# ELU sums, low halves and every second gated product moved off VectorE, and a list scheduler with longer waits, in a top-k attention and two-MLP kernel

## The chip, the cores and the metric

The kernel runs on one core of a Trainium2 chip. The metric is the device time of one execution in microseconds (us). The program has five instruction streams that run side by side and meet only through semaphores: TensorE (PE in the profile; its weight loads are shown apart as PEld), VectorE (DVE), ScalarE (ACT), GpSimd (POOL) and SyncE (SP), which here only issues DMA transfers.

## The reference

Attention that keeps the 32 largest scores of each row, over 4 batches, 8 heads, 576 tokens and a head size of 64, then two MLPs on the 2304 tokens:

```python
scores = scale * q @ k.T
kth = np.partition(scores, -32, axis=-1)[..., -32:-31]
scores = np.where(scores >= kth, scores, -1e9)
attn = softmax(scores)                 # with 1e-9 added to the sum
x = (attn @ v) -> (2304, 512)
h = x @ w_in                           # 512 -> 2048
g = np.where(h > 0, h, np.exp(np.minimum(h, 0)) - 1)     # ELU
x = g @ w_out                          # 2048 -> 512
a, b = x @ w1, x @ w2                  # 512 -> 1024, twice
out = ((a * b) @ w3) @ w_out2          # 1024 -> 1024 -> 512
```

All values are float32.

## The kernel before

**Tiling.** The tokens go in 18 tiles of 128 rows, two tiles to a chunk, so nine chunks (`CHUNKS`). For each chunk there is an attention part and an MLP part; the MLP part of chunk c runs beside the attention part of chunk c+1. After the last attention only the rest of the MLP work is left. Matrix products are made from 16-bit halves: a value is stored as a high half and a low half, and each product takes three matmuls (high by high, high by low, low by high).

**Attention.** For each pair of heads and each tile (72 times) there are: the scores on TensorE (L376, four matmuls for a head, into one PSUM tile `psS`), their copy by ScalarE (L382), the search for the 32nd largest on VectorE (for each head four MAX8, L389, and three MATCH_REPLACE, L392), the masked exponential on ScalarE (L409, L411), the probabilities split into halves by ScalarE (L426) and GpSimd (L427), a transposing DMA (`pt<-pi`), the product with V on TensorE (L442, 28 matmuls), its scaling on VectorE (L447, `xf`, 8 for a chunk), a split by ScalarE (L449) and GpSimd (L450), and a transposing DMA into `x`, the chunk's input to the MLP.

**MLP.** On TensorE a chunk has eight A units (L674 to L676, 24 matmuls of 256 columns each), eight O units (L711 to L713, 24 each), a Y step (the result of O leaves PSUM in halves, L723 and L724, and small matmuls L731 and L736 find its scale), eight B units (L753 to L755, 24 each) and two D units (L788 to L790, 24 matmuls of 512 columns each, the output rows). Between A and O stands the ELU: ScalarE makes Relu(-h) and its exponential (L686, L687), GpSimd subtracts one and scales (L689), and then one of two ways joins the positive branch: VectorE takes the maximum with the PSUM tile (L691), or ScalarE makes a second Relu from PSUM (L695) and GpSimd adds it (L696). ScalarE and GpSimd split the result (L697, L698). In a B unit the two products a and b lie in one PSUM bank; ScalarE copies a (L772) and VectorE multiplies it by b from PSUM (L773), and after every second unit ScalarE and GpSimd split the pair (L778, L779). A second way through the B unit is in the code but not used: ScalarE copies both a and b (L763) and GpSimd multiplies them (L770).

**Weights.** All weights are loaded and unpacked at the start (L474 to L481), and w3 is multiplied by w_out2 on TensorE (L614, 64 matmuls), which gives `w34`. Each of the 56 weight tiles is then converted to a high half by ScalarE (L503) and a low half in one of three ways (`convert`): VectorE alone (mode D, L506), ScalarE scaling in place and GpSimd subtracting (mode G, L509 and L510), or two matmul steps on TensorE (L515 and L516) and a copy by ScalarE (mode P, L518). `conv_modes` takes from `PAR['cd']` how many tiles of a weight go by D and by G; the rest go by P.

**Order.** The order of the instructions on each engine is made when the program is built. Every operation is put in a list (`Program.op`) with an engine, a cost in ns and a priority. `emit` plays the list through: on each engine it takes the ready operation with the lowest rank, where the rank is the priority less `cpw` times the longest path of costs and waits behind the operation:

```python
rank = [o[4] - PAR["cpw"] * cp[i] for i, o in enumerate(self.ops)]
...
rt[s] = max(rt[s], end + (0.0 if e == "SP" else LAT.get((eng, self.ops[s][0]), 130.0)))
```

`LAT` is the wait in ns from the end of an operation on one engine to the start of one on another. On the chip each engine runs its own queue in this order and waits for what its next instruction needs, even when a later one is ready.

Of the kernel before, what the change touches and what calls it, by code (L numbers as in the profile page):

```python
# [36 lines left out]

# [112 lines left out]
def kernel(ctx: ExitStack, tc: tile.TileContext, qd, kd, vd, vn, w_in, w_out, w1, w2, w3t, w4, out,  # L150
# [5 lines left out]
    op = P.op  # L156
# [118 lines left out]
    def norm(pieces, dst, key, pr, kind="rot"):  # L275
# [65 lines left out]
    def attention(c, t0, n):  # L341
# [4 lines left out]
        for pair in range(4):  # L346
            for t in range(n):
# [14 lines left out]
                for hh in range(2):  # L362
# [4 lines left out]
                    for bi, b in enumerate(bs):  # L367
# [51 lines left out]
                for hh in range(2):  # L419
# [81 lines left out]
    def convert(W, nm, i, st, skeys, s, sk, pr, sid, kind="y"):  # L501
# [15 lines left out]
        op("PE", 1080, rest, [*skeys, (nm, i), ("si", sid), "ident"], [pk], pr)  # L517
        op("ACT", 480, lambda: A.activation(lo(W[i]), ps, AF.Copy), [pk], [(nm, i, "l")], pr)  # L518
# [76 lines left out]
    def prep_34(pr):  # L595
# [6 lines left out]
        def part(m):  # L602
# [53 lines left out]
    def mlp(c, t0, n, dprev, pr0, span, hooks=None):  # L656
        xs, vb = c % NXS, batch(t0 + n)
        X = XS[xs]
        N = n * 128
        nm = N / 2.4 + 3.0  # L660
        pr_of = lambda u: pr0 + u * span / 28.0
# [120 lines left out]
        def unitD(t, pr):  # L782
            rs = nxt("rot", 3)
            for q in range(4):
# [128 lines left out]
```

## Time and profile before

| | |
|---|---|
| device time, 3 runs | median 1086.86 us (1085.69 to 1093.07) |
| the profiled execution | 1089.24 us, its span 1087.5 us |
| busy in the span | PE 984.1 us, DVE 921.6, ACT 834.9, POOL 661.2 |
| mean granted TensorE clock | 0.968 of full speed |

The profile is of one execution. The span runs from the first to the last instruction of the program; the device time of the same execution is 1.74 us longer. A matmul's own time in the trace (0.27 us for 256 columns) overlaps with the next ones, since the array works as a pipeline, so TensorE's work is read from the step from one start to the next, not from the durations.

### The profile page before, as it was taken

The numbers are of one execution on the slowest core, as the hardware profiler recorded it, in microseconds if no ns is written. First come the engines' busy times: TensorE is split into PE (matmuls) and PEld (weight loads), VectorE is DVE, ScalarE is ACT, GpSimd is POOL, SyncE is SP. The second block draws the span as 40 slices with busy tenths as digits, with TensorE's granted clock in tenths as the row PEclk, the third lists the DMA queues.
The fourth block names the chain that finished last, engine by engine and source line by source line (L and its number), as shares of the span: only waits on it lengthen the run. The fifth ranks groups of instructions, "written<-read, shape, count | busy, mean of one in ns | idle before, by whom it ended". The sixth has DMA issues, their size and how long they took to land.

```text
span 1087.5 us, 24859 instructions
## 1 busy us (share of the span) xinstructions
PE 984.1 (90%) x9132; PEld 780.0 (72%) x9132; DVE 921.6 (85%) x2002; ACT 834.9 (77%) x1729; POOL 661.2 (61%) x689
## 2 busy tenths in 40 slices
PE   3489847889889999999999999999999999999998
PEld 2244524569678868877886887788879869878875
DVE  6999999899999999999996999998799999951011
ACT  6878797697878867897896798788878967953522
POOL 4898862256357735974794597458738845852711
PEclk9989968799899999999999999999999999999999
DMA  9999996554458895467859657665864563230000
GB/s 363 296 316 316 303 275 169 159 130 112 120 144 163 191 231 149 101 166 198 187 134 237 168 116 144 174 183 124 207 160 113 133 159 81 68 84 11 2 20 20
DMA packets 262298, 174.65 MB, mean 161 GB/s; under 512 B 197408, under 2 KB 224032, under 8 KB 262176
## 3 DMA queue, kind: packets, MB, share of 16 engines
q1 hardware_dynamic: 262176, 173.07, 60.3%
q8 instruction: 71, 1.16, 0.5%
q14 instruction: 51, 0.42, 0.1%
HBM read 104.33 MB, written 21.50 MB: 116 GB/s over the span
## 4 chain that ended last, share of the span: by engine, by line
DVE 22%; PE 14%; ACT 10%; POOL 8%; issue 5%; DMA 5%; SPq 1%; POOLq 0%; ACTq 0%; DVEq 0%
DVE m L389 10%; DVE wk L392 9%; DMA pt<-pi 3%; POOL pi L427 2%; PE psR L753 2%; PE psR L755 2%; PE psR L754 2%; ACT pi L426 2%; POOL g L698 1%; POOL t L696 1%; ACT y L411 1%; ACT s L382 1%; PE psR L788 1%; DMA qr<-qd 1%; PE psR L790 1%
## 5 line engine op out<-in xcount | busy, mean ns | idle before, releaser
L389 DVE MAX8 m<-wk 128x8 f32<-128x576 f32 x432 | 312.5, 747 | 1.3
L427 POOL TENSOR_TENSOR pi<-y,pi 128x576 f16<-128x576 f32 x144 | 188.0, 1314 | 126.6 <-ACT pi L426 96.8
L392 DVE MATCH_REPLACE8 wk<-m,wk 128x576 f32<-128x576 f32 x288 | 212.4, 741 | 0.0
L712 PE MATMUL psY<-g,wout 128*128 128x256 f16 x576 | 157.5, 273 | 1.9 <-POOL g L698 1.9
L753 PE MATMUL psR<-x,w 128*128 128x256 f16 x576 | 158.5, 275 | 0.8 <-DVE t L773 0.8
L754 PE MATMUL psR<-x,w 128*128 128x256 f16 x576 | 158.2, 275 | 1.1 <-DVE x L724 1.1
L674 PE MATMUL psR<-x,win 128*128 128x256 f16 x576 | 158.6, 275 | 0.1
L755 PE MATMUL psR<-x,w 128*128 128x256 f16 x576 | 158.3, 275 | 0.0
L711 PE MATMUL psY<-g,wout 128*128 128x256 f16 x576 | 157.7, 274 | 0.4 <-ACT g L697 0.4
L676 PE MATMUL psR<-x,win 128*128 128x256 f16 x576 | 158.0, 274 | 0.0
L675 PE MATMUL psR<-x,win 128*128 128x256 f16 x576 | 158.0, 274 | 0.0
L713 PE MATMUL psY<-g,wout 128*128 128x256 f16 x576 | 157.6, 274 | 0.0
L376 PE MATMUL psS<-kt,qh 128*128 128x288 f32 x320 | 110.2, 359 | 38.6 <-ACT s L382 19.1
L411 ACT ACTIVATE y<-y,ty 128x576 f32<-128x576 f32 x144 | 110.7, 771 | 3.3 <-POOL ty L401 3.3
L382 ACT ACTIVATE s<-psS 128x576 f32<-128x576 f32 (+1 forms) x160 | 102.3, 640 | 12.3 <-PE psS L376 11.4
L409 ACT ACTIVATE y<-s,ty 128x576 f32<-128x576 f32 x144 | 107.1, 769 | 5.4 <-POOL pi L427 2.1
L389 DVE MAX8 m<-s 128x8 f32<-128x576 f32 x144 | 105.1, 746 | 6.4 <-ACT s L382 6.0
L392 DVE MATCH_REPLACE8 wk<-m,s 128x576 f32<-128x576 f32 x144 | 106.3, 741 | 0.0
L376 PEld LDWEIGHTS psS<-kt,qh 128*128 128x128 f32 x320 | 63.4, 198 | 54.5 <-ACT s L382 24.7
L442 PE MATMUL psA<-vv,pt 128*128 128x64 f16 (+1 forms) x2240 | 84.1, 196 | 17.2 <-DMA pt<-pi 17.1
L442 PEld LDWEIGHTS <-pt 128*128 128x128 f16 (+1 forms) x2240 | 77.6, 103 | 29.8 <-DMA pt<-pi 20.4
L426 ACT ACTIVATE pi<-y 128x576 f16<-128x576 f32 x144 | 95.2, 677 | 3.8 <-DMA pt<-pi 3.4
(167 smaller groups left out, 2426.8 us busy)
## 6 DMA issues: line engine op xcount, KB each, us to landing
kt<-kd SPq DMA_DIRECT2D x64, 288.0 KB, 3.3
vv<-vd SPq DMA_DIRECT2D x32, 448.0 KB, 4.6
qr<-qd SPq DMA_DIRECT2D x72, 128.0 KB, 3.0
raw<-kd SPq DMA_DIRECT2D x32, 288.0 KB, 4.2
kd<-kt SPq DMA_DIRECT2D x32, 288.0 KB, 3.9
wout<-w_in SPq DMA_DIRECT2D x16, 512.0 KB, 8.3
w<-w3t SPq DMA_DIRECT2D x16, 512.0 KB, 7.0
w<-w_out SPq DMA_DIRECT2D x16, 512.0 KB, 6.2
```

Source lines behind the costliest of these rows:

```text
L376: T.matmul(psS[:, half, 0:288], lhsT=L[qs][:, hh], rhs=KT[kk][:, half * 288:half * 288 + 288], start=li == 0, stop=li == 1)
L389: op("DVE", 685, lambda r=r, src=src, m8=m8, hh=hh: V.max(m8[:, hh, 8 * r:8 * r + 8], src), [skey], [mk], p1 + PAR["ot"] * STEP)
L392: op("DVE", 677, lambda r=r, nsrc=nsrc, w=w, m8=m8, hh=hh: V.match_replace(w, m8[:, hh, 8 * r:8 * r + 8], nsrc, -3.0e38), [skey, mk], [k], ...
L427: op("POOL", 1234, lambda Y=Y, PIs=PIs: G.tensor_tensor(PIs[:, S:2 * S], Y, PIs[:, 0:S], op=OP.subtract), [yk], [("pi", ps)], p4 + .034 * ...
L442: T.matmul(psA[c0:c1, hs], lhsT=PT[pts[hh]][:, j, c0:c1], rhs=W[vs][:, j, hs], start=i == 0, stop=i == 13)
L674: T.matmul(o, lhsT=hi(W)[:, cs], rhs=X[:, 0, kd_, 0:N], start=kd_ == 0, stop=False)
L675: T.matmul(o, lhsT=hi(W)[:, cs], rhs=X[:, 1, kd_, 0:N], start=False, stop=False)
L676: T.matmul(o, lhsT=lo(W)[:, cs], rhs=X[:, 0, kd_, 0:N], start=False, stop=kd_ == 3)
L711: T.matmul(o, lhsT=hi(W)[:, cs], rhs=rh, start=ft == 0 and m % 2 == 0, stop=False, skip_group_check=True)
L753: T.matmul(o, lhsT=hi(W)[:, cs], rhs=X[:, 0, kd_, 0:N], start=kd_ == 0, stop=False)
L754: T.matmul(o, lhsT=hi(W)[:, cs], rhs=X[:, 1, kd_, 0:N], start=False, stop=False)
L755: T.matmul(o, lhsT=lo(W)[:, cs], rhs=X[:, 0, kd_, 0:N], start=False, stop=kd_ == 3)
```

## The change

The diff touches numbers only; every way through the code that is used after it was there before.

- `PAR['cd']`: of the 8 tiles of `w34`, the low halves were all made by VectorE; now 4 by ScalarE and GpSimd and 4 by TensorE and ScalarE. Of the 16 tiles of `w12`, all by VectorE before; now 8 by VectorE and 8 by ScalarE and GpSimd.
- `gm0`, `gm1` (the ELU of chunks 0 and 1): from VectorE's maximum to the second Relu and GpSimd's add, as the other seven chunks have it.
- `bm` = 2: in B units 0, 2, 4 and 6 of every chunk ScalarE copies a and b and GpSimd multiplies.
- `LAT`: ten of the waits between two engines are 1.8 times as long; the waits within an engine and those to SP stay.
- Costs in the list: among others MAX8 685 to 665, MATCH_REPLACE 677 to 727, scores 640 to 560, the transposing DMA 1008 to 1050, DMA rate 360 to 325. All priorities in `PAR` have new values, and `cpw` goes from 13 to 231. These change the order alone.

```diff
-LAT = {("ACT", "PE"): 285.0, ("POOL", "PE"): 210.0, ("DVE", "PE"): 200.0, ("PE", "ACT"): 197.0, ("PE", "DVE"): 197.0, ("ACT", "ACT"): 153.0,
+LAT = {("ACT", "PE"): 513.0, ("POOL", "PE"): 378.0, ("DVE", "PE"): 360.0, ("PE", "ACT"): 355.0, ("PE", "DVE"): 355.0, ("ACT", "ACT"): 153.0,
...
-PAR = dict(whole=('w12',), cd={'wi': [0, 0], 'wo': [0, 0], 'w34': [8, 0], 'w12': [16, 0]}, pv=116.655, pi=265.308, p34=113.061, po=180.969, p12=190.557, pis=199.858,
+PAR = dict(whole=('w12',), cd={'wi': [0, 0], 'wo': [0, 0], 'w34': [0, 4], 'w12': [8, 8]}, pv=305.528, pi=344.478, p34=-139.464, po=377.719, p12=-289.232, pis=887.934,
...
-           nr34=2, gm0=0, gm1=0, gm=1, bm=0, cpw=13.0, step=6600.0, pvb=-52.296)
+           nr34=2, gm0=1, gm1=1, gm=1, bm=2, cpw=231.477, step=6600.0, pvb=-215.647)
...
-        op("SP", nbytes / 360.0, lambda: Q.dma_start(dst, src), r, w, pr, lat=475.0)
+        op("SP", nbytes / 325.0, lambda: Q.dma_start(dst, src), r, w, pr, lat=475.0)
...
-                        op("PE", 640, qk, [("qh", qs), ("ql", qs), ("k", kk)], ["psS"], p1 + PAR["os"] * STEP)
+                        op("PE", 560, qk, [("qh", qs), ("ql", qs), ("k", kk)], ["psS"], p1 + PAR["os"] * STEP)
...
-                        op("DVE", 685, lambda r=r, src=src, m8=m8, hh=hh: V.max(m8[:, hh, 8 * r:8 * r + 8], src), [skey], [mk], p1 + PAR["ot"] * STEP)
+                        op("DVE", 665, lambda r=r, src=src, m8=m8, hh=hh: V.max(m8[:, hh, 8 * r:8 * r + 8], src), [skey], [mk], p1 + PAR["ot"] * STEP)
```

Three places show the new order. The first is on TensorE at the start, where the first product with V (`psA<-vv`) stands behind the first matmuls of w3 by w_out2 (`psY<-w,pp`). Before:

```order
L286 LDWEIGHTS win
L286 MATMUL psR_174<-win 128x128
L614 MATMUL psY_170<-w_115,pp 128x512 x8
L442 LDWEIGHTS pt_142
L442 MATMUL psA<-vv_128,pt_142 128x64
```

And in the changed program:

```order
L286 MATMUL psR_174<-win 128x128
L614 MATMUL psY_170<-w_115,pp 128x512 x5
L614 MATMUL psY_171<-w_115,pp 128x512 x8
L614 MATMUL psY_170<-w_115,pp 128x512 x3
L442 LDWEIGHTS pt_142
L442 MATMUL psA<-vv_128,pt_142 128x64
```

Sixteen of the 64 matmuls stand ahead of it now, eight before.

The second is on ScalarE at the first A units of chunk 0 (`t` is the ELU's buffer, `psR` the PSUM bank of an A unit, `wout` a weight tile in conversion). Before:

```order
L686 ACTIVATE t_146<-psR_172,sc 128x512
L686 ACTIVATE t_147<-psR_173,sc 128x512
L687 ACTIVATE t_146<-t_146 128x512
L503 ACTIVATE wout<-wout,sc 128x512 x2
L518 ACTIVATE wout<-psY_171 128x512
L518 ACTIVATE wout<-psY_170 128x512
L400 ACTIVATE ty_165<-m_161 128x2
L687 ACTIVATE t_147<-t_147 128x512
L409 ACTIVATE y_138<-s_134,ty_165 128x576
```

And in the changed program:

```order
L686 ACTIVATE t_146<-psR_172,sc 128x512
L686 ACTIVATE t_148<-psR_173,sc 128x512
L687 ACTIVATE t_146<-t_146 128x512
L518 ACTIVATE wout<-psY_171 128x512
L695 ACTIVATE t_147<-psR_172,sc 128x512
L503 ACTIVATE wout<-g_153,sc 128x512
L518 ACTIVATE wout<-psY_170 128x512
L687 ACTIVATE t_148<-t_148 128x512
L695 ACTIVATE t_149<-psR_173,sc 128x512
L697 ACTIVATE g_151<-t_146 128x512
```

The second Relu (L695) of each A unit has come into ScalarE's queue, and attention's L400 and L409 stand further back.

The third is on GpSimd in the B units of chunk 1, where `pp` are the gated products in halves and `pi` attention's probabilities. Before:

```order
L779 TENSOR_TENSOR pp<-t_148,pp 128x2x256
L401 TENSOR_TENSOR ty_164<-m_160 128x2
L450 TENSOR_TENSOR xt_155<-xf_156,xt_155 128x128
L779 TENSOR_TENSOR pp<-t_149,pp 128x2x256
L427 TENSOR_TENSOR pi_140<-y_138,pi_140 128x576
```

And in the changed program:

```order
L770 TENSOR_TENSOR t_149<-t_148 128x256
L401 TENSOR_TENSOR ty_164<-m_160 128x2
L770 TENSOR_TENSOR t_146<-t_150 128x256
L779 TENSOR_TENSOR pp<-t_149,pp 128x2x256
L427 TENSOR_TENSOR pi_140<-y_138,pi_140 128x576
L450 TENSOR_TENSOR xt_155<-xf_156,xt_155 128x128
L357 TENSOR_TENSOR ql_123<-qr,qh_121 128x256
L427 TENSOR_TENSOR pi_141<-y_139,pi_141 128x576
L770 TENSOR_TENSOR t_148<-t_147 128x256
L779 TENSOR_TENSOR pp<-t_146,pp 128x2x256
```

One multiply (L770) stands ahead of each split of a pair (L779), between the instructions of attention.

## Rows read from the trace of the kernel before

**Rows 1.** The page's head: span, and TensorE's and VectorE's busy time.

```profile
span 1087.5 us, 24859 instructions
...
PE 984.1 (90%) x9132; PEld 780.0 (72%) x9132; DVE 921.6 (85%) x2002; ACT 834.9 (77%) x1729; POOL 661.2 (61%) x689
```

**Rows 2.** Windows: length, busy PE, PEld, DVE, ACT, POOL, clock, DMA share, GB/s.

```profile
0.00:205.40 205.40, 138.45 (x706) 75.94 (x707) 184.07 (x354) 159.84 (x306) 136.96 (x113) 0.88 0.93 287
205.40:324.10 118.70, 105.72 (x996) 86.33 (x995) 116.06 (x265) 100.56 (x205) 57.31 (x64) 0.95 0.45 117
324.10:963.60 639.50, 619.96 (x6424) 523.42 (x6424) 606.96 (x1348) 531.66 (x1142) 429.11 (x475) 0.99 0.64 155
963.60:1087.50 123.90, 119.96 (x1012) 94.28 (x1009) 14.55 (x37) 42.85 (x78) 37.82 (x38) 1.00 0.07 20
199.50:319.70 120.20, 109.58 (x998) 86.79 (x997) 116.98 (x271) 100.34 (x205) 57.31 (x64) 0.95 0.47 124
```

**Rows 3.** Timeline of TensorE: start, duration, what; steps between starts are its pace.

```profile
204.26 1.12 PE L515 MATMUL psY<-wout,si 128*128 128x512 f32 x2
...
205.44 0.27 PE L674 MATMUL psR<-x,win 128*128 128x256 f16 x1
...
324.05 0.44 PE L674 MATMUL psR<-x,win 128*128 128x256 f16 x1
...
953.36 0.38 PE L376 MATMUL psS<-kt,qh 128*128 128x288 f32 x1
...
953.98 1.04 PE L442 MATMUL psA<-vv,pt 128*128 128x64 f16 x28
954.85 0.27 PE L674 MATMUL psR<-x,win 128*128 128x256 f16 x1
...
956.16 0.27 PE L711 MATMUL psY<-g,wout 128*128 128x256 f16 x1
...
961.40 0.38 PE L788 MATMUL psR<-w,pp 128*128 128x512 f16 x1
...
962.70 0.27 PE L711 MATMUL psY<-g,wout 128*128 128x256 f16 x1
...
1083.35 0.38 PE L790 MATMUL psR<-w,pp 128*128 128x512 f16 x1
```

**Rows 4.** Waits on TensorE between 330 and 965 us, the two longest: total, times, longest.

```profile
PE psA L442 <- DMA pt<-pi: 10.7, 15, 2.1
PE psS L376 <- ACT s L382: 5.4, 8, 1.4
```

**Rows 5.** Timeline of VectorE: the last `xf` of chunks 0 and 1.

```profile
199.50 0.27 DVE L447 TENSOR_TENSOR xf<-psA,ty 128x128 f32<-128x128 f32 x1
...
319.67 0.27 DVE L447 TENSOR_TENSOR xf<-psA,ty 128x128 f32<-128x128 f32 x1
```

**Rows 6.** Groups of VectorE: count, busy us, mean ns, idle before.

```profile
L773 DVE SCALAR_TENSOR_TENSOR t<-psR,sc,t 128x256 f32<-128x256 f32 x72 | 34.0, 475 | 34.5 <-ACT t L772 34.3
L506 DVE SCALAR_TENSOR_TENSOR w<-w,sc 128x512 f16<-128x512 f32 x21 | 16.3, 801 | 0.2 <-ACT w L503 0.2
L691 DVE SCALAR_TENSOR_TENSOR t<-psR,sc,t 128x512 f32<-128x512 f32 x16 | 11.7, 739 | 2.2 <-POOL t L689 2.2
L475 DVE SCALAR_TENSOR_TENSOR w<-pp,w 128x512 int32<-128x512 int32 x10 | 7.1, 707 | 0.0
```

**Rows 7.** The same groups of ScalarE.

```profile
L695 ACT ACTIVATE t<-psR,sc 128x512 f32<-128x512 f32 x56 | 38.2, 682 | 0.4 <-POOL g L698 0.4
L772 ACT ACTIVATE t<-psR,sc 128x256 f32<-128x256 f32 x72 | 33.6, 466 | 39.2 <-PE psR L755 35.0 <-DVE sc L263 4.0
```

**Rows 8.** The same of GpSimd.

```profile
L696 POOL TENSOR_TENSOR t<-t,t 128x512 f32<-128x512 f32 x56 | 71.4, 1276 | 2.3
```

**Rows 9.** Timeline of VectorE: the shortest kind and a long one of L479.

```profile
28.67 0.67 DVE L479 SCALAR_TENSOR_TENSOR w<-w 128x512 int32<-128x512 int32 x1
...
46.09 1.78 DVE L479 SCALAR_TENSOR_TENSOR w<-w 128x512 int32<-128x512 int32 x1
```

More of the change, by code (lines that the diff above doesn't have):

```diff
@@ L23 @@
 DM, DFF, DH = 512, 2048, 1024
-CHUNKS = [2]*9
-LAT = {("ACT", "PE"): 285.0, ("POOL", "PE"): 210.0, ("DVE", "PE"): 200.0, ("PE", "ACT"): 197.0, ("PE", "DVE"): 197.0, ("ACT", "ACT"): 153.0,
-       ("ACT", "DVE"): 147.0, ("ACT", "POOL"): 175.0, ("DVE", "ACT"): 128.0, ("DVE", "DVE"): 127.0, ("DVE", "POOL"): 203.0, ("POOL", "ACT"): 75.0,
-       ("POOL", "DVE"): 60.0, ("POOL", "POOL"): 88.0, ("PE", "PE"): 0.0, **{(e, "SP"): 67.0 for e in ("PE", "ACT", "DVE", "POOL")}}
+CHUNKS = [2] * 9
+LAT = {("ACT", "PE"): 513.0, ("POOL", "PE"): 378.0, ("DVE", "PE"): 360.0, ("PE", "ACT"): 355.0, ("PE", "DVE"): 355.0, ("ACT", "ACT"): 153.0,
+       ("ACT", "DVE"): 265.0, ("ACT", "POOL"): 315.0, ("DVE", "ACT"): 230.0, ("DVE", "DVE"): 127.0, ("DVE", "POOL"): 365.0, ("POOL", "ACT"): 135.0,
+       ("POOL", "DVE"): 108.0, ("POOL", "POOL"): 88.0, ("PE", "PE"): 0.0, **{(e, "SP"): 67.0 for e in ("PE", "ACT", "DVE", "POOL")}}
 NXS = 2
 STEEP = 2.0 ** 100
-PAR = dict(whole=('w12',), cd={'wi': [0, 0], 'wo': [0, 0], 'w34': [8, 0], 'w12': [16, 0]}, pv=116.655, pi=265.308, p34=113.061, po=180.969, p12=190.557, pis=199.858,
-           pos=-94.236, p12s=-194.985, p34s=16.277, ci=202.374, co=66.783, cos=-57.999, c12=275.249, m34=-471.595, c34=-63.018, m34s=28.657, h34=2, oq=53.713, os=7.994,
-           ok=113.472, ot=242.797, orr=151.048, opp=-250.875, oa=-82.219, ost=0.618, a0=125.007, a1=-15.227, lag0=114.106, lag=21.439, ho=2, h12=0, h12c=7,
-           nr34=2, gm0=0, gm1=0, gm=1, bm=0, cpw=13.0, step=6600.0, pvb=-52.296)
+PAR = dict(whole=('w12',), cd={'wi': [0, 0], 'wo': [0, 0], 'w34': [0, 4], 'w12': [8, 8]}, pv=305.528, pi=344.478, p34=-139.464, po=377.719, p12=-289.232, pis=887.934,
+           pos=-39.975, p12s=-141.369, p34s=-39.306, ci=627.574, co=250.52, cos=-285.263, c12=456.68, m34=-949.454, c34=-1036.071, m34s=-404.56, h34=2, oq=135.113, os=23.084,
+           ok=482.279, ot=801.632, orr=1285.509, opp=-504.17, oa=-189.735, ost=-530.322, a0=192.434, a1=69.385, lag0=120.972, lag=-77.615, ho=2, h12=0, h12c=7,
+           nr34=2, gm0=1, gm1=1, gm=1, bm=2, cpw=231.477, step=6600.0, pvb=-215.647)
 def conv_modes(n, d, g):
@@ L286, in gram @@
                     T.matmul(ps[0:w, o:o + w], lhsT=c, rhs=c, start=pi == 0 and j == 0, stop=pi == len(pieces) - 1, skip_group_check=True)
-            op("PE", 55 * (n + 127) // 128, gram, keys, [pk], pr)
+            op("PE", 70 * (n + 127) // 128, gram, keys, [pk], pr)
         op("DVE", 600, lambda: V.tensor_reduce(m, ps, axis=AX.X, op=OP.max), [pk], ["nm0"], pr)
@@ L388, in attention @@
                         src, skey = (sS, ("s", ss)) if r == 0 else (w, k)
-                        op("DVE", 685, lambda r=r, src=src, m8=m8, hh=hh: V.max(m8[:, hh, 8 * r:8 * r + 8], src), [skey], [mk], p1 + PAR["ot"] * STEP)
+                        op("DVE", 665, lambda r=r, src=src, m8=m8, hh=hh: V.max(m8[:, hh, 8 * r:8 * r + 8], src), [skey], [mk], p1 + PAR["ot"] * STEP)
                         if r < 3:
                             nsrc = sS if r == 0 else w
-                            op("DVE", 677, lambda r=r, nsrc=nsrc, w=w, m8=m8, hh=hh: V.match_replace(w, m8[:, hh, 8 * r:8 * r + 8], nsrc, -3.0e38),
+                            op("DVE", 727, lambda r=r, nsrc=nsrc, w=w, m8=m8, hh=hh: V.match_replace(w, m8[:, hh, 8 * r:8 * r + 8], nsrc, -3.0e38),
                                [skey, mk], [k], p1 + PAR["ot"] * STEP)
@@ L428, in attention @@
                        [yk], [("pi", ps)], p4 + .034 * STEP)
-                    op("SP", 1008, lambda PIs=PIs, pt=pt: Q.dma_start_transpose(out=PT[pt], in_=PIs), [("pi", ps)], [("pt", pt)], p4 - 1e6, lat=1406.0)
+                    op("SP", 1050, lambda PIs=PIs, pt=pt: Q.dma_start_transpose(out=PT[pt], in_=PIs), [("pi", ps)], [("pt", pt)], p4 - 1e6, lat=1406.0)
                 if t == 0:
@@ L516, in rest @@
             T.matmul(ps, lhsT=nident, rhs=hi(W[i]), start=False, stop=True)
-        op("PE", 1080, rest, [*skeys, (nm, i), ("si", sid), "ident"], [pk], pr)
+        op("PE", 1250, rest, [*skeys, (nm, i), ("si", sid), "ident"], [pk], pr)
         op("ACT", 480, lambda: A.activation(lo(W[i]), ps, AF.Copy), [pk], [(nm, i, "l")], pr)
@@ L613, in part @@
                     k = a * 4 + kk
-                    op("PE", 860, lambda w=w3[a][0], kk=kk, k=k: T.matmul(acc, lhsT=w[:, kk * 128:kk * 128 + 128], rhs=W4[k][0], start=k == 0, stop=k == 7),
+                    op("PE", 930, lambda w=w3[a][0], kk=kk, k=k: T.matmul(acc, lhsT=w[:, kk * 128:kk * 128 + 128], rhs=W4[k][0], start=k == 0, stop=k == 7),
                        w3[a][1] + W4[k][1], [ak], p1)
@@ L659, in mlp @@
         N = n * 128
-        nm = N / 2.4 + 3.0
+        nm = N / 2.4 + 3.2
         pr_of = lambda u: pr0 + u * span / 28.0
@@ L791, in unitD @@
                 ks = [("pp", 2 * q), ("pp", 2 * q + 1), ("w34", 2 * q), ("w34", 2 * q + 1)]
-                op("PE", 1305, mm, ks + [k + ("l",) for k in ks], [("rot", rs)], pr)
+                op("PE", 1325, mm, ks + [k + ("l",) for k in ks], [("rot", rs)], pr)
             ts = nxt("t2", NT2)
```

2 lines of the change are left out of this document (1 added, 1 removed).

## The prediction

> **What bounds the kernel now.** I read the page's head first, then windows cut at the kernel's own landmarks, then the pace of TensorE, then its waits. The head shows two engines that are nearly full, TensorE at 90% and VectorE at 85% of the span, with ScalarE at 77% and GpSimd at 61% [rows 1]. Such shares are means over stages, so the windows decide. From the start to the first A unit of chunk 0 (A0, 205.4 us) VectorE is busy 184 us and TensorE much less; from A0 to the first A unit of chunk 1 (A1, 324 us) VectorE is busy 116 of 119 us; from A1 to the end of attention TensorE is busy 620 of 640 us and VectorE 607; after it TensorE 120 of 124 us and the others little [rows 2]. So VectorE sets the pace at the start, and TensorE sets it later, with VectorE close behind.
>
> How much of TensorE's time is work? Its pace where it doesn't wait is read from starts [rows 3]: 12 matmuls of 256 columns take 1.31 us (954.85 to 956.16), 6 of 512 columns 1.30 us (961.40 to 962.70), a head's 4 score matmuls 0.62 us, 28 matmuls with V 0.87 us, one low half by mode P (L515, L516) 1.18 us (204.26 to 205.44). The order puts behind A1 4608 matmuls of A, O and B (503.0 us), 432 of D (93.6), 119 heads of scores (73.8), 64 groups with V (55.7), and some 110 small ones, at half of a 256-column one or a little more 8.6 us: 734.7 us. It ran from 324.05 to 1083.57 (the last start plus 0.22) [rows 3], 759.5 us. So **24.8 us after A1** are lost. The granted clock, 0.99 in the long window, is some 6 us of that [rows 2]; the two longest waits are 10.7 us for the transposed probabilities and 5.4 us for ScalarE to empty the score tile [rows 4]. From A0 to A1 the order holds about 100.2 us of work and 118.6 passed: 18.4 us lost, 5.9 of them by the clock of 0.95 (5% of 118.7) [rows 2].
>
> I take therefore three terms: when A0 can start, how long A0 to A1 takes, and what is lost after A1. TensorE's own work behind A1 hardly changes.
>
> **The change part by part.** *What VectorE sheds.* 16 maxima of the ELU at 739 ns (11.8 us), 36 gated products at 475 ns (17.1 us) and 16 low halves at 801 ns (12.8 us) [rows 6]: 41.7 us, or some 37 without the ends that overlap the next instruction.
>
> *What the others get.* ScalarE: 16 second Relus at 682 ns (10.9), 36 copies that are twice as wide (682 in place of 466 ns, 7.8), 12 scalings in place and 4 evacuations, at most 682 ns each (10.9) [rows 7]: under 30 us. GpSimd: 16 adds at 1276 ns (20.4), 36 multiplies of 256 columns, for which there is no row, and I take half of the 512-column add (23.0), 12 subtractions at no more than the add (15.3) [rows 8]: under 59 us. It is busy 57 us of 119 between A0 and A1 and 429 of 640 later [rows 2], so the sum lies beside other work as long as its queue isn't blocked. TensorE: 4 low halves at 1.18 us, 4.7 us [rows 3], ahead of A1 where it has idle time; at worst all of it counts.
>
> *A0.* It needs the eighth `xf` of chunk 0 (199.50) and the transfer behind it; A0 came 5.9 us after [rows 3, 5]. In the changed order VectorE has ahead of that `xf` 8 fewer low halves (-6.4 us), but two more whole-word unpackings of three instructions at up to 707 ns (up to +4.2) and one more MAX8 [rows 6]. Between -6.4 and -1.5 I take -4: VectorE is busy 184 of 205 us there [rows 2], and where it idles others set the pace. `xf` at 195.5, A0 at 201.4. A load can't take the gain away wholly: the order of the transfers is nearly the same, with 72 weight loads ahead of the same place.
>
> *A0 to A1.* VectorE was busy 117.0 of the 120.2 us between the last `xf` of chunk 0 and that of chunk 1 [rows 2, 5], 97%: this stretch is its own. It sheds 8 low halves (6.4), 8 maxima (5.9) and 4 products (1.9); by the order some top-k steps move in and unpackings out, so I count 107 us. But ScalarE gets here 8 second Relus and 8 scalings (10.9 us) [rows 7] and gives up about 1: 100.3 becomes 110 us [rows 2]. TensorE has about 99 us, and 105 with the clock. So **ScalarE is late next**. At VectorE's 97% the 110 us take 113; ScalarE also waits for others (VectorE's share was reached with work that was ready), so I take 115, with 110 (107 at 97%, ScalarE full) and 131 (ScalarE's present share, 100.3 of 120.2) as the ends. The next `xf` is then at 310.5, and A1, which came 4.4 us after [rows 3, 5], at **315** in place of 324.
>
> *After A1.* The order leaves 734.3 us of work on TensorE, one head of scores fewer. VectorE sheds 28 products (13.3) and 8 maxima (5.9) of its 607 us [rows 2, 6]: 588, or 92% of the window in place of 95%. The new waits in the list also put more of TensorE's other work between a producer and its use at the Y step: from the last O matmul to L731 8 to 10 us in place of 6 to 9, and from L731 to L736 5 in place of 1.6 to 3 us, worked out from the two orders at the pace above. For attention the distance from scores to V stays at 30 us on average. I take a third off the 24.8 us: 17. The ends are 6 (the clock's part alone) and 30 (more waiting on GpSimd than now).
>
> *The end.* The last D matmul ends 3.9 us before the span does [rows 1, 3]; nothing in the last stage moves but the gated products, whose multiply of 0.64 us fits in the 2.6 us of a B unit.
>
> The sum: 315 + 734.3 + 17 + 3.9 = 1070.2 us of span, against 1087.5. The execution was 1.7 us longer than its span, and 2.4 us above the median of the runs: **1069.5 us**.
>
> **A rule that speaks against it.** VectorE's unpacking step L479, with both inputs in SBUF, takes 0.67 us in one place and 1.78 in another [rows 9], while GpSimd works beside it. The Trainium skill, page "SBUF — State Buffer", section "Who interferes with whom", says that such an instruction and a GpSimd instruction that reads SBUF shut each other out, the second waiting for the first, and that an instruction with one SBUF input does not. "Perfetto Trace Analysis", section "Optimizing Scalar/DVE Operations", draws from it that moving work between the two might not help. The removed maxima and products read PSUM and one SBUF tile, so by that rule they never collided, and what takes their place on GpSimd can.
>
> **The rivals.**
> (1) *GpSimd's new instructions hold VectorE up.* If each of the 8 subtractions for `w12` between A0 and A1 stops VectorE for its full 1.28 us, VectorE has 117 us again, the stretch takes 120, and A1 comes at 320: 1075 us. For it speaks the 1.78 us of L479 [rows 9], against it that all unpackings are behind VectorE by then and it mostly runs top-k steps with one input tile.
> (2) *The waits stay.* A0 is set by the same loads and A0 to A1 by a chain, not by VectorE's sum; after A1 TensorE waits for transfers whose time nobody changes [rows 4]. Then only the 4.7 us of mode P can show: 1087 to 1092 us. For it speaks a DMA share of 0.93 up to A0 [rows 2].
> (3) *Slower: ScalarE becomes the bound of the start.* The first product with V stands behind 16 in place of 8 matmuls of w3, some 7 us later, and ScalarE's second Relus stand ahead of attention's L400 and L409. If that puts the last `xf` of chunk 0 10 us later than it was (209.5) and ScalarE keeps its 83% in the next stretch (131 us), A1 comes at 345, and with 20 us lost the time is 345 + 734.3 + 20 + 3.9 - 0.7 = 1102 us. It decides from an A1 of 340 on. Against it: ScalarE idles 45 us ahead of A0 [rows 2], so it has room to catch up.
> (4) *More gain.* ScalarE runs full, A1 comes at 310, and only the clock's 6 us are lost: 1053 us.
>
> **How the numbers follow.** Forecast 0.41, (1) 0.12, (2) 0.17, (3) 0.15, (4) 0.15. A measurement of this kernel tells about 1% from no change, that is under 1076 and over 1098 us. The forecast and (4) are faster, (1) lies on the line and is halved: 0.62 faster, 0.23 within, 0.15 slower. The range of 1050 to 1094 leaves out the far part of (4) and nearly all of (3), under 0.2.
>
> **What the profile after would show.** A0 near 201 and A1 near 315; between the last `xf` of chunks 0 and 1 ScalarE over 90% busy and VectorE under 97%; VectorE's sum near 885 us, GpSimd's near 718, ScalarE's near 863; TensorE's waits after A1 for `pt` and `psS` smaller, and 17 us lost there. Wrong would be an A1 later than 324 (then by what ScalarE waited for), or TensorE waiting after A1 for L698 or L770, or an A0 set by a weight load.

## The result and the profile after

The changed kernel takes 1075.28 us (median of 7 runs, 1071.49 to 1081.83), the kernel before 1087.96 us beside it (7 runs, 1085.69 to 1094.48). The ratio is 0.9874, with an interval of 0.9847 to 0.99: 1.3% faster. One sentence ahead of the prediction has to be mended: the weights come as 64-bit floats, which is why they are unpacked.

The profile after is of the execution of 1081.83 us, the longest of the seven, so what it shows is 6.5 us longer than the median. First the page's head and the windows, cut at the same landmarks and with the columns of [rows 2]; the last window runs from the last `xf` of chunk 0 to that of chunk 1.

```profile
span 1079.9 us, 24952 instructions
...
PE 980.6 (91%) x9144; PEld 777.7 (72%) x9144; DVE 897.6 (83%) x1934; ACT 858.2 (79%) x1761; POOL 725.4 (67%) x753
```

```profile
0.00:216.10 216.10, 144.49 (x725) 78.13 (x726) 184.93 (x337) 167.08 (x318) 146.39 (x118) 0.91 0.88 275
216.10:329.80 113.70, 103.57 (x994) 84.75 (x993) 110.80 (x261) 108.14 (x221) 79.70 (x83) 0.97 0.49 121
329.80:968.50 638.70, 624.80 (x6500) 528.01 (x6500) 592.99 (x1312) 540.36 (x1150) 455.99 (x507) 1.00 0.64 154
968.50:1079.90 111.40, 107.70 (x932) 86.78 (x929) 8.90 (x27) 42.64 (x75) 43.29 (x45) 1.00 0.09 25
212.00:325.00 113.00, 102.44 (x962) 81.77 (x961) 110.10 (x261) 106.75 (x217) 77.61 (x82) 0.97 0.50 123
```

The landmarks on TensorE's timeline (first A unit of chunk 0, of chunk 1, last D matmul) and on VectorE's (last `xf` of chunks 0 and 1), which answer to [rows 3, 5]:

```profile
216.08 0.27 PE L674 MATMUL psR<-x,win 128*128 128x256 f16 x1
...
329.76 0.28 PE L674 MATMUL psR<-x,win 128*128 128x256 f16 x1
...
1075.83 0.38 PE L790 MATMUL psR<-w,pp 128*128 128x512 f16 x1
```

```profile
212.04 0.27 DVE L447 TENSOR_TENSOR xf<-psA,ty 128x128 f32<-128x128 f32 x1
...
325.02 0.29 DVE L447 TENSOR_TENSOR xf<-psA,ty 128x128 f32<-128x128 f32 x1
```

TensorE's two waits of [rows 4], between 330 and 970 us:

```profile
PE psA L442 <- DMA pt<-pi: 10.9, 17, 1.4
PE psS L376 <- ACT s L382: 1.7, 3, 0.7
```

By the three terms: A0 is at 216.1 where 201.4 was forecast, and later than before (205.4). A0 to A1 takes 113.7 us; 113.6 was forecast, 118.7 it took before. From A1 to the last matmul's end (1075.83 plus 0.22) are 746.3 us; less the prediction's 734.3 us of work, 12.0 are lost, where 17 were forecast and 24.8 were lost before. The tail is 3.9 us as before. So the span's 1079.9 is the forecast's 1070.2 plus 14.7 at the start, plus 0.1, less 5.0 at the end. Against before, the start loses 10.7 us, A0 to A1 gains 5.0 and the part behind A1 12.8.

Why A0 is late stands in VectorE's time ahead of the last `xf` of chunk 0: 180.9 us busy and 31.2 idle, against 178.7 and 20.8 before. The windows up to that `xf`, first before, then after (columns of [rows 2]):

```profile
0.00:199.50 199.50, 132.62 (x695) 73.88 (x696) 178.74 (x340) 155.71 (x299) 136.53 (x112) 0.89 0.94 289
```

```profile
0.00:212.04 212.04, 140.86 (x715) 76.86 (x716) 180.87 (x327) 163.70 (x311) 145.76 (x116) 0.91 0.88 276
```

VectorE's longest waits from 11 us to that `xf`, first before, then after (what waited, for whom: us in total, times, longest):

```profile
DVE xf L447 <- PE psA L442: 2.7, 4, 1.2
DVE w L479 <- ACT w L478: 2.6, 3, 1.8
DVE w L474 <- DMA pp<-w: 2.4, 3, 1.2
```

```profile
DVE w L479 <- ACT w L478: 9.5, 13, 2.3
DVE w L474 <- DMA pp<-w: 4.9, 3, 3.7
```

The waits of L479 and L474 together grew by 9.4 us, nearly all of the 10.4 us more that VectorE idles. L474 waits for a load itself. VectorE's unpacking step L479 stands behind ScalarE's L478, and ScalarE's L478 now stands behind loads. The group rows of L478 (count, busy us, mean ns, idle before and what ended it), before and after:

```profile
L478 ACT ACTIVATE w<-w 128x512 int32<-128x512 uint32 x40 | 27.0, 674 | 5.1 <-DMA w<-w_out 2.9 <-POOL pi L427 1.3 <-DMA w<-w 0.7
L478 ACT ACTIVATE wout<-wout 128x512 int32<-128x512 uint32 x16 | 10.7, 666 | 0.0
```

```profile
L478 ACT ACTIVATE w<-w 128x512 int32<-128x512 uint32 x40 | 26.7, 670 | 12.3 <-DMA w<-w_out 7.3 <-DMA w<-w3t 3.7 <-POOL pi L427 1.3
L478 ACT ACTIVATE wout<-wout 128x512 int32<-128x512 uint32 x16 | 10.8, 674 | 4.1 <-DMA wout<-w_in 4.1
```

Loads held L478 up for 3.6 us before and for 15.1 us after, though the same bytes are loaded: in the new order the unpacking step comes to the head of ScalarE's queue before its load has landed.

VectorE's busy total fell by 24.0 us (921.6 to 897.6), not by 37. Part of the difference is that some instructions at new places took longer. VectorE's groups, after, and the two that [rows 6] lacks, before:

```profile
L329 DVE SCALAR_TENSOR_TENSOR vv<-raw,sc,vv 128x640 f16<-128x640 f32 x16 | 20.1, 1257 | 2.3 <-ACT vv L326 2.3
...
L506 DVE SCALAR_TENSOR_TENSOR w<-w,sc 128x512 f16<-128x512 f32 x7 | 7.1, 1009 | 0.1
...
L474 DVE TENSOR_SCALAR w<-w 128x512 int32<-128x512 int32 x4 | 3.6, 925 | 0.0
```

```profile
L329 DVE SCALAR_TENSOR_TENSOR vv<-raw,sc,vv 128x640 f16<-128x640 f32 x16 | 18.0, 1128 | 1.3 <-ACT vv L326 1.2
...
L474 DVE TENSOR_SCALAR w<-w 128x512 int32<-128x512 int32 x4 | 1.6, 416 | 0.0
```

All three have their inputs in SBUF. Those that read PSUM kept their time (L773: 475 ns before, 474 after). GpSimd's new work, after (16 of the 72 adds L696 are new):

```profile
L696 POOL TENSOR_TENSOR t<-t,t 128x512 f32<-128x512 f32 x72 | 93.3, 1296 | 3.2 <-ACT t L695 1.2
L770 POOL TENSOR_TENSOR t<-t 128x256 f32<-128x256 f32 x36 | 26.7, 745 | 41.6 <-ACT t L763 41.3
L510 POOL TENSOR_TENSOR w<-w 128x512 f16<-128x512 f32 x11 | 14.5, 1316 | 5.2 <-ACT w L509 4.8 <-DVE xf L447 0.4
```

### The profile page after: what moved, and what is told of

It reads as the page before. It is cut to its first block, busy times and chain, and to the rows that moved or that the text cites. A ratio compares the mean times of both kernels' runs of the same rounds, so it can differ in the third digit from the quotient of the medians.

```text
span 1079.9 us, 24952 instructions
## 1 busy us (share of the span) xinstructions
PE 980.6 (91%) x9144; PEld 777.7 (72%) x9144; DVE 897.6 (83%) x1934; ACT 858.2 (79%) x1761; POOL 725.4 (67%) x753
## 4 chain that ended last, share of the span: by engine, by line
PE 34%; DVE 26%; ACT 14%; DMA 10%; POOL 8%; issue 6%; SPq 1%; POOLq 0%; DVEq 0%; ACTq 0%
DVE m L389 11%; DVE wk L392 10%; DMA pt<-pi 5%; PE psR L753 3%; PE psR L754 3%; PE psR L755 3%; PE psR L674 2%; PE psR L675 2%; PE psR L676 2%; PE psS L376 2%; PE psA L442 2%; POOL pi L427 2%; PE psY L711 2%; PE psY L712 2%; PE psY L713 2%
## 5 line engine op out<-in xcount | busy, mean ns | idle before, releaser
L427 POOL TENSOR_TENSOR pi<-y,pi 128x576 f16<-128x576 f32 x144 | 190.7, 1332 | 121.6 <-ACT pi L426 88.0
L389 DVE MAX8 m<-s 128x8 f32<-128x576 f32 x144 | 105.7, 747 | 17.6 <-ACT s L382 17.3
L409 ACT ACTIVATE y<-s,ty 128x576 f32<-128x576 f32 x144 | 107.4, 771 | 4.9 <-POOL pi L427 1.6
L696 POOL TENSOR_TENSOR t<-t,t 128x512 f32<-128x512 f32 x72 | 93.3, 1296 | 3.2 <-ACT t L695 1.2
```

The source lines that it names most:

```text
L389: op("DVE", 665, lambda r=r, src=src, m8=m8, hh=hh: V.max(m8[:, hh, 8 * r:8 * r + 8], src), [skey], [mk], p1 + PAR["ot"] * STEP)
L427: op("POOL", 1234, lambda Y=Y, PIs=PIs: G.tensor_tensor(PIs[:, S:2 * S], Y, PIs[:, 0:S], op=OP.subtract), [yk], [("pi", ps)], p4 + .034 * ...
```

## The experiments

The theory after the result: the relief of VectorE pays from A0 on, and the start is lost to waits on loads that the list's order brings; the moves and the list's numbers belong together. Its rivals: the list alone makes the gain, the moves alone make it, GpSimd's subtractions or the late first product with V make the start late.

One table for all, from each kernel's profiled execution. "Lost" is TensorE's time from A1 on less its work there by the kernel's own order at the prediction's pace, good to some 3 us, so that a -3 counts as none. Ratios are to the kernel before, run on the same chip.

| kernel | ratio (95%) | median us | A0 | A1 | lost after A1 |
|---|---|---|---|---|---|
| before | 1 | 1087.96 | 205.4 | 324.1 | 25 |
| after | 0.9874 (0.9847 to 0.99) | 1075.28 | 216.1 | 329.8 | 12 |
| m1_moves | 1.0851 (1.079 to 1.0913) | 1177.9 | 301.2 | 427.6 | 30 |
| m2_list | 1.0052 (1.0028 to 1.0077) | 1091.62 | 218.9 | 354.3 | 1 |
| m3_lat1 | 1.0166 (1.0116 to 1.0216) | 1104.86 | 242.7 | 346.3 | 19 |
| m5_lat18 | 1.0128 (1.0082 to 1.0174) | 1105.43 | 242.0 | 340.5 | 22 |
| m4_dve | 1.011 (1.0068 to 1.0152) | 1099.13 | 218.6 | 339.6 | 20 |
| m6_prod | 0.9946 (0.9921 to 0.997) | 1084.66 | 215.4 | 328.2 | 12 |
| m7_elulo | 0.9972 (0.994 to 1.0003) | 1088.1 | 219.4 | 338.5 | 9 |
| m8_av | 0.9885 (0.9841 to 0.993) | 1078.78 | 219.1 | 331.8 | 8 |
| m9_no476 | 0.98 (0.9762 to 0.9837) | 1069.66 | 212.0 | 322.4 | 8 |
| m11_nosub | 0.9878 (0.9848 to 0.9908) | 1077.55 | 217.1 | 330.0 | 11 |
| m12_land17 | 0.9792 (0.9742 to 0.9843) | 1065.77 | 204.9 | 321.3 | 8 |
| m13_land25 | 0.9686 (0.9644 to 0.9729) | 1053.59 | 201.2 | 321.2 | 0 (-3) |

**The moves without the list (m1_moves).** The kernel before, with the moves alone:

```diff
-cd={..., 'w34': [8, 0], 'w12': [16, 0]}, ... gm0=0, gm1=0, gm=1, bm=0, cpw=13.0
+cd={..., 'w34': [0, 4], 'w12': [8, 8]}, ... gm0=1, gm1=1, gm=1, bm=2, cpw=13.0
```

> The kernel before with the three moves alone (12 low halves by GpSimd and 4 by TensorE, the ELU of chunks 0 and 1, every second gated product); waits, costs and priorities of the list stay as before. Theory R (relief: the gain after A1 comes because VectorE, shed of some 37 us, delivers earlier): nearly the whole gain, ratio 0.987 to 0.99 (1074 to 1077 us), TensorE's loss after A1 falls from 25 to 12-16 us. Theory L (list: the gain comes because the order leaves more time between a producer and its use on TensorE): ratio 0.998 to 1.005, loss after A1 stays at 22 us or more.

It is 8.5% slower. Windows of 50 us at the start (columns of [rows 2]) and TensorE's longest waits in the whole run:

```profile
150.00:200.00 50.00, 19.21 (x146) 13.59 (x146) 46.44 (x91) 28.91 (x63) 19.81 (x23) 0.53 0.68 173
200.00:250.00 50.00, 21.06 (x178) 16.70 (x178) 48.91 (x110) 30.71 (x70) 21.83 (x27) 0.50 0.55 137
```

```profile
PE psA L442 <- DMA pt<-pi: 61.4, 45, 5.9
PE psS L376 <- ACT s L382: 49.6, 31, 8.7
```

TensorE is busy for two fifths of these windows at a granted clock of 0.5, its lower level, and waits for attention's transfers and for ScalarE. VectorE has 9 us less to do than before (912.5 against 921.6), and the time is 91 us longer: the order decides here, not the engines' sums. Neither theory had this: both expected a ratio of 1.005 or less.

**The list without the moves (m2_list).** The changed kernel, with the moves undone and its waits, costs and priorities kept:

```diff
-cd={..., 'w34': [0, 4], 'w12': [8, 8]}, ... gm0=1, gm1=1, gm=1, bm=2, cpw=231.477
+cd={..., 'w34': [8, 0], 'w12': [16, 0]}, ... gm0=0, gm1=0, gm=1, bm=0, cpw=231.477
```

> The changed kernel with the three moves undone: VectorE has its 16 maxima, 36 products and 16 low halves back, waits, costs and priorities of the list stay as changed. Theory R: the gain is gone, 1085 to 1092 us against 1088 before, loss after A1 over 20 us. Theory L: 1074 to 1079 us, loss after A1 10 to 16 us.

It is 0.5% slower than before. The window from A0 to A1 and TensorE's longest wait in it:

```profile
218.90:354.30 135.40, 114.77 (x1085) 91.76 (x1084) 132.19 (x301) 116.03 (x239) 65.38 (x74) 0.90 0.54 130
```

```profile
PE psS L376 <- ACT s L382: 16.8, 6, 11.1
```

A1 comes late here, 27.3 us behind the last `xf` of chunk 1 (327.03) where it came 4.7 us behind it after: four heads of scores and three groups with V more stand ahead of A1 on TensorE, and 26 more top-k steps on VectorE (15.2 us). Little is lost behind A1. Where the order shifts, A1 and the loss behind it aren't two separate terms, and only their sum can be compared. What stands is the total: the list alone gives no gain, as the relief theory had it, but without the loss after A1 that this theory expected.

**The factor by itself (m3_lat1, m5_lat18).** The changed kernel with the waits of before, and the kernel before with the waits of after. The edit of m3_lat1, which m5_lat18 makes the other way round:

```diff
-LAT = {("ACT", "PE"): 513.0, ("POOL", "PE"): 378.0, ...
+LAT = {("ACT", "PE"): 285.0, ("POOL", "PE"): 210.0, ...
```

> The changed kernel with the waits of the list as before (1.0 in place of 1.8 times); moves, costs and priorities as changed. Theory L in its narrow form (the factor 1.8 itself does it): 1083 to 1090 us with a loss after A1 of 20 us or more. Theory R: 1073 to 1079 us.

> The kernel before with the ten waits of the list 1.8 times as long and nothing else (no moves, costs and priorities as before). If the longer waits by themselves make TensorE wait less: the loss after A1 falls from 25 to 5-15 us, and the time to 1070-1080 us where the start stays as it is. If the priorities belong to the waits that they were found with: the loss after A1 may fall, but the start loses 15 us or more (as the changed kernel's start did with the old waits), 1085 to 1110 us.

Both are slower than before, by 1.7% and 1.3%, and both have A0 at 242. The first lies outside what either theory expected, the second where the priorities belong to their waits. The changed kernel loses 3.0% with the shorter waits (1.0166 over 0.9874), the kernel before loses 1.3% with the longer ones. The priorities fit one list, and a list with other numbers under the same priorities is another order. So no worth of the factor by itself can be told.

**The relief with the order held (m4_dve, m6_prod, m7_elulo).** The changed kernel, its list untouched; at build time the instruction is given to VectorE in the same place. m4_dve has all three edits, m6_prod the product alone, m7_elulo the other two (of each line the call alone is shown):

```diff
-G.tensor_tensor(t, T2[tb][:, 0:N], T2[tb][:, N:2 * N], op=OP.mult)
+V.tensor_tensor(t, T2[tb][:, 0:N], T2[tb][:, N:2 * N], op=OP.mult)
...
-G.tensor_tensor(t, t, t2a, op=OP.add)
+(V if c < 2 else G).tensor_tensor(t, t, t2a, op=OP.add)
...
-G.tensor_tensor(lo(W[i]), st, hi(W[i]), op=OP.subtract)
+V.tensor_tensor(lo(W[i]), st, hi(W[i]), op=OP.subtract)
```

> The changed kernel with every queue in its order, but the 36 multiplies, the 16 adds of chunks 0 and 1 and the 12 subtractions that the change gave to GpSimd made by VectorE from the same SBUF tiles at the same place (64 instructions, an estimated 33 us by the 475 to 801 ns of its like). Theory R: A1 5 to 15 us later and more loss after it, 1084 to 1100 us. Theory L: within 5 us of the changed kernel, up to 1080 us.

> The changed kernel with every queue in its order, but the 36 multiplies of the gated products by VectorE (from the same SBUF tiles, 36 x 0.45 to 0.5 us = 16 to 18 us, 4 of them in each chunk); the ELU and the low halves stay with GpSimd. If the relief of the later chunks is what counts: loss after A1 from 12 to 17-20 us, the start unchanged, 1080 to 1086 us. If VectorE has room there (93% busy after A1): within 3 us of the changed kernel.

> The changed kernel with every queue in its order, but the 16 adds of the ELU of chunks 0 and 1 and the 12 subtractions by VectorE (28 instructions of 0.7 to 0.8 us, some 20 us, all ahead of the end of chunk 1's MLP); the products stay with GpSimd. If the start is VectorE's: A1 8 to 14 us later and the whole 8 to 14 us longer, 1083 to 1090 us. If ScalarE or the transfers set the start: under 4 us.

What VectorE then does in m4_dve, by groups, and its window from A0 to A1:

```profile
L770 DVE TENSOR_TENSOR t<-t 128x256 f32<-128x256 f32 x36 | 19.2, 535 | 13.4 <-ACT t L763 13.3
...
L696 DVE TENSOR_TENSOR t<-t,t 128x512 f32<-128x512 f32 x16 | 13.6, 851 | 0.0
...
L510 DVE TENSOR_TENSOR w<-w 128x512 f16<-128x512 f32 x11 | 8.4, 766 | 0.0
```

```profile
218.60:339.60 121.00, 104.18 (x993) 85.25 (x991) 120.52 (x280) 108.82 (x220) 59.67 (x63) 0.97 0.44 113
```

These 41.2 us on VectorE cost 2.4% (1.011 over 0.9874), some 26 us: A0 2.5 us later, A0 to A1 7.3 us longer, with VectorE busy 120.5 of 121.0 us, and 8 us more lost behind A1 (17.3 us more span in all, since the profiled execution of after is its longest). The products alone are worth 0.7%, the adds and subtractions 1.0%, with A1 8.8 us later. With the order held, VectorE is the bound from A0 to A1. The profiled run of m6_prod was its fastest of ten and shows no more loss after A1 than after (12), where 17 to 20 were expected, so where its 0.7% lies isn't shown.

**The first products with V (m8_av).** The changed kernel, with the first two groups with V moved ahead of the L614 matmuls that stand before each, nothing else moved (850 is the list's cost of such a group, 930 that of L614's):

```diff
         order.sort()
+        at = [i for _, i in order]
+        av = sorted(i for i in range(n) if self.ops[i][0] == "PE" and self.ops[i][1] == 850)[:2]
...
+            while self.ops[pe[j - 1]][1] == 930:
+                j -= 1
...
+            at.insert(at.index(pe[j]), i)
```

> The changed kernel with two groups of 28 matmuls moved on TensorE's queue alone: the first product with V stands ahead of the first 16 matmuls of w3 by w_out2 (its operands landed at 45 us, it ran at 64.7), the second ahead of the next 19 (landed at 83, ran at 104.5). If their late place is what holds A0 back (216 us against 205 before): A0 at 205 to 212 and 4 to 10 us gained. If VectorE's queue and its waits for loads set A0: A0 within 3 us, time unchanged.

The two products start at 48.4 and 85.5 us here, at 64.7 and 104.5 after; the first started at 53.2 before. The ratio is 0.9885, A0 219.1: A0 isn't earlier, so their late place costs nothing.

**Less on VectorE, nothing on others (m9_no476).** The changed kernel without the third of the three whole-word steps:

```diff
-op("DVE", 602, lambda: V.scalar_tensor_tensor(d, low, 29, d, op0=OP.logical_shift_right, op1=OP.bitwise_or), ...)
+op("DVE", 602, lambda: None, ...)
```

> The changed kernel with every queue in its order, but without the last step (L476) of the 16 whole-word unpackings, which leaves the three lowest bits of w1 and w2 out: 16 instructions of 0.69 us fewer on VectorE, 14 of them (9.7 us) ahead of the last xf of chunk 0. If VectorE's sum sets A0 and A1: A0 at 206 to 211 in place of 216, A1 6 to 11 us earlier, 1064 to 1069 us. If the weight loads and ScalarE's steps behind them set A0: A0 within 4 us of 216, VectorE's idle time ahead of it 35 us or more in place of 31.

The window from the start to A0:

```profile
0.00:212.00 212.00, 146.47 (x724) 79.56 (x725) 178.66 (x323) 167.65 (x319) 143.21 (x118) 0.91 0.90 281
```

VectorE has 6.6 us less ahead of the last `xf` of chunk 0 and idles 2.2 us more there (33.3), A0 is 4.0 us earlier and A1 7.4, and the ratio falls to 0.98. This lies between the two cases expected. Three fifths of the relief at the start come through, so VectorE's work counts there as well, but its waits of over 30 us stay.

**GpSimd's subtractions taken away (m11_nosub).**

```diff
...
-A.activation(st, st, AF.Copy, scale=s)
+A.activation(lo(W[i]) if nm == "w12" else st, st, AF.Copy, scale=s)
-G.tensor_tensor(lo(W[i]), st, hi(W[i]), op=OP.subtract)
+None if nm == "w12" else G.tensor_tensor(lo(W[i]), st, hi(W[i]), op=OP.subtract)
```

> The changed kernel with every queue in its order, but without GpSimd's 8 subtractions for w12, which stand between A0 and A1: the low halves of these 8 tiles of w1 and w2 become a copy of the scaled tile made by ScalarE in the same time, so that the output is not exact. If GpSimd's new instructions hold VectorE up there (rival 1 of the prediction): the stretch from A0 to A1 is up to 10 us shorter. If they lie beside other work: A1 within 2 us, time within 0.3%.

The ratio is 0.9878 and A1 comes at 330.0: the eight subtractions cost nothing.

**A list that reckons with later landings (m12_land17, m13_land25).** The changed kernel; the list lets a transfer land 1700 or 2500 ns after it has moved, and all priorities in `PAR` were chosen anew for that list. Work, moves and `LAT` are as after. Three lines fewer, so L474 to L479 are L471 to L476, and L447 is L444. The edit of m12_land17 (2500.0 in m13_land25):

```diff
                 dma = begin + cost
-                end = dma + 900.0
+                end = dma + 1700.0
```

> The changed kernel's moves and waits, but the list reckons that a transfer lands 1.7 us after its last byte in place of 0.9, and the priorities were fitted anew to that list. If the start is lost because VectorE's and ScalarE's unpacking steps stand in their queues before their loads have landed (L479 after L478 after the load: 9.5 us of VectorE's 31 us idle ahead of A0): VectorE's idle time ahead of the last xf of chunk 0 falls to 26 us or less, A0 comes at 200 to 210 us, 1060 to 1070 us. If the load waits are not the lever: A0 after 213, 1073 to 1090 us.

> The same with 2.5 us in place of 0.9, priorities fitted anew to that. If longer landing is the lever: idle time ahead of the last xf of chunk 0 under 24 us, 1058 to 1070 us. If the list then holds VectorE's other work back too much: A0 after 213, 1073 to 1090 us.

Both beat the changed kernel: 0.9792 and 0.9686. VectorE idles 12.6 and 15.2 us ahead of the last `xf` of chunk 0 in place of 31.2. The second is faster than its expectation had it. In m13_land25, the page's head, the windows to A0, to A1 and from there to 940 us, and VectorE's longest waits from 11 to 199.5 us:

```profile
span 1053.0 us, 24951 instructions
...
PE 973.4 (92%) x9144; PEld 774.5 (74%) x9144; DVE 900.5 (86%) x1934; ACT 856.1 (81%) x1761; POOL 722.4 (69%) x753
```

```profile
0.00:201.20 201.20, 135.56 (x743) 74.79 (x744) 186.03 (x349) 165.03 (x321) 144.95 (x121) 0.95 0.93 286
201.20:321.20 120.00, 112.02 (x1041) 88.37 (x1039) 119.51 (x263) 115.61 (x235) 84.64 (x86) 0.95 0.57 143
321.20:940.00 618.80, 616.63 (x6445) 523.81 (x6443) 586.18 (x1299) 536.68 (x1144) 452.64 (x506) 1.00 0.66 158
```

```profile
DVE xf L444 <- PE psA L439: 3.0, 1, 3.0
DVE w L476 <- ACT w L475: 2.4, 5, 1.5
```

VectorE has as much to do as after (900.5 and 897.6 us), yet is 92% busy up to A0 (86% after) and all but full from A0 to A1. Its wait for ScalarE's unpacking is down from 9.5 to 2.4 us, that for loads is no longer among its waits, and TensorE waits for `pt` once, for 0.9 us, between 300 and 950:

```profile
PE psA L439 <- DMA pt<-pi: 0.9, 1, 0.9
```

How much of it is the landing time and how much the new priorities isn't separated: no kernel has priorities chosen anew with the landing time left at 900 ns.

## Why the prediction was right in its total, and wrong at the start

**The total** was 1069.5 for 1075.28 us, within its range, with faster as the likeliest case. The profiled execution shows that two errors offset each other in part, 14.7 us lost ahead of A0 and 5.0 gained behind A1, so that some of the nearness is luck. Two of the three signs that the prediction gave for being wrong came: A1 is later than 324 (329.8), and weight loads hold up the work ahead of A0. The third did not: TensorE waited 0.3 us in all for L698 after A1 and not for L770.

**A0, the step that failed.** The prediction took 4 us off VectorE's work ahead of the last `xf` of chunk 0, left its idle time as it was and came to 201.4. Measured is 216.1. VectorE's busy time there rose by 2.1 us in place of falling by 4 (+6.1), its idle time rose by 10.4, and A0 followed the `xf` after 4.0 us in place of 5.9 (-1.9): together the 14.7 us, to rounding. "A load can't take the gain away wholly" was the wrong sentence: it looked at the order of the transfers, which hardly changed, and not at where their users stand. (By the traces 70 of the 72 weight loads were issued ahead of chunk 0's last transfer into `x` before and 71 after, where it counted 72.) Loads held L478 up 11.5 us more. That the waits can be taken out with the same work is shown by m12_land17 and m13_land25 (idle 12.6 and 15.2 us), though both have new priorities as well. The busy time was mis-sized in the unpackings: the eight low halves are gone from there as forecast, but L474 to L476 take 29.3 us ahead of that `xf` in place of 21.6, where the prediction allowed up to 4.2 more for two more unpackings. L474 alone went from 5.1 to 9.4 us, twelve before and fourteen after.

Such collisions were weighed, but in the wrong stage: for the subtractions from A0 to A1, not for the unpackings ahead of A0. The prediction's rule for instructions with one SBUF input also left out an exception. The Trainium skill, "SBUF — State Buffer", section "Who interferes with whom", says that `tensor_scalar` with its operand in SBUF can take the port pair shared with GpSimd, and that a VectorE instruction with two SBUF inputs shuts GpSimd's reads out and is shut out by them. The traces agree: one L474 took 0.40 us at best and 1.51 at worst after, L479 0.67 and 1.78 [rows 9], while L773 with its PSUM input never changed.

**A0 to A1** was right to 0.1 us, but not for its reason. The prediction made ScalarE the late one, with 110 us against VectorE's 107. Measured between the two `xf` are 110.1 of 113.0 us on VectorE, 97%, and 106.75 on ScalarE, 94%: VectorE stays the fuller engine, and m4_dve shows it as the bound. That the two sizes changed places and the length still came out is luck. What ScalarE's share costs wasn't tried by a kernel.

**After A1** the direction was right and the size too small: 12.0 us lost in place of 17. `psS` fell from 5.4 to 1.7 us and the granted clock rose to 1.00, but the wait for `pt` stayed (10.7 and 10.9 us), though the prediction expected both to shrink. With the relief undone (m4_dve), 8 of the 12.8 us gained here are lost again.

**The busy sums.** VectorE 897.6 (885 forecast), ScalarE 858.2 (863), GpSimd 725.4 (718). GpSimd's multiply took 745 ns, where half of the add, 638, was taken.

**The rivals.** (1), GpSimd's subtractions, would give 1075 us, the time measured, but not for its reason: m11_nosub leaves them out and nothing moves. (2), the waits stay, is right in that loads hold up the start, but it falls by the loss after A1, halved, and by m4_dve, where VectorE's sum sets A0 to A1. (3), slower, would decide from an A1 of 340; it came at 329.8, and m8_av shows that the late products cost nothing. (4)'s time is what m13_land25 reaches with the same work, 1053.6 us, but not its way: A1 is at 321.2 there, not at 310, under another list. What no case held: that the change isn't a sum of its parts. The moves alone cost 8.5%, the list alone 0.5%, and together they gain 1.3%.

**Still open:** where the 6.5 us lie by which the profiled execution is longer than the median (the late A0 is no trait of that execution: m6_prod, m8_av and m11_nosub, with nearly the same orders, have it at 215.4 to 219.1); what the landing time and the priorities each do in m13_land25; and why hardly anything is lost after A1 there.

## What to carry to other kernels

A prediction from busy sums holds inside a stage where one engine is full; in a stage that also waits for loads, look up where each load's user stands in the new order, not only where the load stands. When a list scheduler's numbers change, its priorities belong to them: an edit is judged with the order held (the same place, another engine) or with priorities made for it, and a mixture of old and new tells nothing. If profiles show users waiting for transfers, a list that reckons with longer landings, with priorities made for it, is worth trying before more work is taken off engines.

## What the runs showed of the hardware that was not expected

VectorE and GpSimd can hold each other up by more than the length of an instruction, and this holds for a VectorE instruction with a single SBUF input too. Two such instructions (L474, a shift and a mask) before, and two after, followed by what GpSimd did beside the latter (start, us, what):

```profile
167.46 0.75 DVE L474 TENSOR_SCALAR w<-w 128x512 int32<-128x512 int32 x2
```

```profile
154.31 2.80 DVE L474 TENSOR_SCALAR w<-w 128x512 int32<-128x512 int32 x2
```

```profile
153.80 1.60 POOL L510 TENSOR_TENSOR w<-w 128x512 f16<-128x512 f32 x1
155.36 1.47 POOL L481 TENSOR_TENSOR wout<-wout,w 128x512 int32<-128x512 int32 x1
```

The pair took 2.80 us in place of 0.75, and L510 beside it 1.60 us, where its mean is 1.32. Each of the two L474 ends 0.28 us after GpSimd's L510 and L481 (155.40 and 156.83). GpSimd loses more where VectorE's unpackings stand in a row, in the first row before, in the second after:

```profile
167.67 4.11 POOL L481 TENSOR_TENSOR g<-g,w 128x512 int32<-128x512 int32 x1 [0.75 <-ACT win L518]
```

```profile
168.17 5.69 POOL L427 TENSOR_TENSOR pi<-y,pi 128x576 f16<-128x576 f32 x1 [2.25 <-ACT pi L426]
```

The L481 just ahead of the first row took 1.30 us, and L427's mean is 1.33. Both end 1.1 to 1.2 us after the last of the VectorE steps L474 to L476 that run in a row beside them (170.61 and 172.72). What this costs A0 isn't shown. That these rows shut each other out is inferred from their overlap; no run took the one away and kept the other.
